# A norm, local attention, norm and gated feed-forward layer: one rank for every step, attention weights divided before they are spread, and five norms named for transposes by DMA

## The chip, the cores and the metric

The kernel runs on one core of a Trainium2 chip. The metric is the time of one execution on the device in microseconds (us); before the change the median of five runs is 211.15 us (211.06 to 212.95). A core has a matmul engine (TensorE, PE in the profile; PEld is its loading of weights), a vector engine (VectorE, DVE), an engine for activation functions and copies (ScalarE, ACT), GpSimd (POOL) and a queue engine (SyncE, SP) that issues DMAs. Each executes its own instructions in order and waits for the others by semaphores. Matmuls write to PSUM, which has eight banks of 128 partitions by 512 fp32 values; all other tiles lie in SBUF.

## What is computed

The input `x` has 2048 positions of width 512. The layer is pre-norm attention, then a pre-norm gated feed-forward, each with a residual. B_x is not used.

```python
h  = x + A(layernorm(x))
h2 = h + B(layernorm(h))

# A: 32 heads of width 16; each position attends to 8 positions: itself, 2 back, ... 14 back
q, k, v = split(x @ wqkv)
logits = einsum("bhsd,bhswd->bhsw", q, kg) * 16**-0.5     # kg, vg: k, v at s - 2*w
attn = softmax(where(s - 2*w >= 0, logits, -1e9))
A = einsum("bhsw,bhswd->bhsd", attn, vg) @ wo

# B: F = 1376
gate = x @ W_gate; gate = gate * (gate > 0)
B = (gate * (x @ W_up)) @ W_down
```

Data are bf16; layernorm has no weights and an epsilon of 1e-5.

## The kernel before

The positions are cut into four chunks of 512 (`tk` 0 to 3), each of four blocks of 128 rows. Row-wise work (norms, residuals, output) has positions on the partitions, all other work has features on the partitions and the 512 positions along the free dimension, so each norm's output is transposed. A chunk passes through these steps:

- **Norm of x** (`layernorm`, L400): DVE takes mean and variance of each block (L429, L432), ACT makes the reciprocal deviation by Ln and Exp (L442, L446), then DVE (chunk 0) or ACT (L484) writes the normed block. Four PE transposes a block write to PSUM (L494, 16 for a norm), and two ACT copies for a chunk bring two blocks each to SBUF (L512; one of chunk 0 is on DVE, L510). A second branch of the function transposes by DMA from SP (`f_td`, four transfers a block); it is entered on the test `(ln, tk) in DMAT` at L458, where `ln` is "x" or "h" and `tk` the chunk, and `DMAT` is the empty tuple.
- **Projections**: twelve groups of four matmuls (L544) for q, k and v, each drained by ACT (L552). In chunk 0 the first two groups are cut in half-widths, so that they can start on half the rows.
- **Scores**: DVE multiplies q with four shifted views of k for two feature tiles at a time (L591, four instructions a chunk). Eight small matmuls sum within heads (L597, four groups a chunk). ACT takes the exponential (L606), four window positions in each of two tiles; in chunk 0 DVE zeroes what lies before the start (L609).
- **Weights**: the undivided exponentials are spread by PE from a head to its features (L625, two groups of four) and copied by ACT to SBUF (L632, eight). Beside this two matmuls give the sums (L639), and ACT makes their reciprocal by Ln (L642) and Exp (L645).
- **Values**: for each of four feature tiles DVE multiplies the eight spread weights with shifted views of v (L662), adds eight to one in three steps (L665) and multiplies with the reciprocal (L669, tile `rec`).
- **Output product and residual**: four groups of four matmuls (L700); DVE adds each to x and keeps the sum of each row (L705).
- **Norm of h**: from these sums (L414), ACT's square sums (L420), Ln, Exp, DVE (L487), transposes as above.
- **Feed-forward**: 11 feature tiles, the last of 96; for each four matmuls for up and four for gate (L727), two ACT drains (L731, L734), a DVE product for two tiles (L747). Then for each block 11 matmuls in two parts of 8 and 3 (L759), a DVE addition of h (L763) and a store from SP.

The order is not the program's. Each step is added to a `Plan` (L168) with an engine, an estimated duration, its dependencies and the buffers that it takes. `Plan.order` (L189) then makes the order before the kernel is built: for each engine it collects the steps that could start soonest, within a small window (`LOOK`: 0.05 us for PE, 0.3 DVE, 0.1 ACT), and takes the one with the smallest priority. The priorities come from the table `PRIO`: one number for each kind of step and chunk (L182). Buffers are given out in the same pass: 8 PSUM banks for all uses, 9 tiles `quad` for normed, projected and attended data, 5 tiles `big` for products and weights. The engines receive their steps in the resulting order and keep it.

Input loads are issued in a fixed order in `setup`: x of chunk 0 (half from SP, half from ACT), the three projection weights, x of chunk 1, wo, up and gate weights, x of chunks 2 and 3, the down weights. While the first rows load, 54 matmuls on zeros (`NWARM`, L522) keep PE busy.

Of the kernel before, what the change touches and what calls it, by code (L numbers as in the profile page):

```python
# [8 lines left out]
P = 128  # L9
# [8 lines left out]
PRIO = {  # L18
    "warm": (329, 0, 0, 0),
    "xst": (-357, -495, 2394, -54),  # L20
    "xag": (-520, -862, -182, 1996),
    "xrl": (-362, -296, 194, 2166),
    "xre": (-82, 283, 2306, 886),
    "xxn": (-286, 2378, 367, 2013),
    "xtp": (540, 1594, 641, 716),
    "xte": (-646, 2834, 2727, 2443),
    "qkh0": (442, 0, 0, 0),
    "qkv0": (418, 417, 1697, 353),
    "qe0": (1262, 2340, 2135, 2291),
    "qkh1": (1644, 0, 0, 0),  # L30
    "qkv1": (449, 1372, 2578, 2742),
    "qe1": (2915, 2429, 2602, -366),
    "qkv2": (352, 2556, 1012, 1671),
    "qe2": (2725, 402, 863, 106),
    "qkv3": (453, 1501, 226, 815),
    "qe3": (2462, 2595, 2528, 2174),
    "qkv4": (1443, 695, 1687, 267),
    "qe4": (-122, 2839, 177, 2325),
    "qkv5": (701, 873, 594, 1878),
    "qe5": (-44, -211, -170, 2493),  # L40
    "qkv6": (862, 1457, 638, 395),
    "qe6": (-199, -327, 2260, -230),
    "qkv7": (487, 427, 68, 358),
    "qe7": (402, 2319, 2485, -311),
    "qkv8": (1720, 1667, 1519, 453),
    "qe8": (2802, 2488, 2656, 114),
    "qkv9": (1851, -242, 2722, 391),
    "qe9": (1309, 2749, 876, 2302),
    "qkv10": (1764, 857, 1851, 1678),
    "qe10": (2412, 1400, 2395, 458),  # L50
    "qkv11": (2427, 1522, 1794, 722),
    "qe11": (2598, 2825, -204, 2326),
    "pr0": (-482, 1697, -427, 2119),
    "sc0": (1698, 2659, 1551, 1498),
    "ex0": (2396, 2052, 1825, -25),
    "mk0": (2108, 0, 0, 0),
    "pr1": (-469, 1768, -500, 2606),
    "sc1": (404, 855, 418, 1193),
    "ex1": (1517, 142, -363, 143),
    "mk1": (-591, 0, 0, 0),  # L60
    "bc0": (1924, 469, 3082, 309),
    "be0": (-60, -227, 44, 2335),
    "bc1": (-281, 491, 1693, 187),
    "be1": (-373, 324, 2173, 119),
    "den": (1891, 635, 1806, 811),
    "dl": (2476, 2727, -37, 2595),
    "dr": (2494, 2236, 2409, 3002),
    "mu0": (-490, -741, -300, -559),
    "tree0": (-169, -269, -240, -508),
    "om0": (1670, 1359, 1810, -68),  # L70
    "mu1": (-422, -682, -366, -477),
    "tree1": (-140, -329, -243, -384),
    "om1": (-229, -267, 2395, -350),
    "mu2": (-555, -491, 2098, -268),
    "tree2": (-170, 1809, -660, 904),
    "om2": (-521, 1855, -320, -517),
    "mu3": (-551, 1681, 1796, 1815),
    "tree3": (-437, 1819, -540, 1964),
    "om3": (1672, 1855, -287, 2080),
    "wo0": (627, 1946, 489, 2577),  # L80
    "rs0": (-246, -458, -830, -312),
    "wo1": (438, 583, 385, 3140),
    "rs1": (-643, 2078, 1855, 2067),
    "wo2": (313, 69, 182, 553),
    "rs2": (-732, -369, -32, 1663),
    "wo3": (1166, 959, 49, 924),
    "rs3": (-414, -240, 1839, -148),
    "hnm": (-209, -423, 2603, -326),
    "hsq": (2388, 2706, 2324, -39),
    "hrl": (-604, -445, 2636, -334),  # L90
    "hre": (2395, -231, 2261, 2466),
    "hxn": (-412, -519, -293, -471),
    "htp": (609, 1635, 1868, 152),
    "hte": (1320, 2163, 155, 494),
    "mm0": (1484, 427, 528, 389),
    "ue0": (-673, 2837, 2251, 2336),
    "ge0": (44, 2326, -675, 97),
    "gu0": (2058, -433, -474, -124),
    "mm1": (823, 1820, 930, -289),
    "ue1": (1892, 191, 2067, -310),  # L100
    "ge1": (2639, 225, 2423, 2049),
    "gu1": (-496, -252, 1690, -742),
    "mm2": (-16, 412, 2609, 908),
    "ue2": (2776, 2713, -363, 2679),
    "ge2": (-65, 2678, 2266, 2262),
    "gu2": (2019, -373, -285, 1530),
    "mm3": (1801, -279, -278, 2624),
    "ue3": (2151, 164, 2100, 2147),
    "ge3": (-79, 2604, 224, -393),
    "gu3": (-491, -577, -568, 1516),  # L110
    "mm4": (471, 1194, -255, 2655),
    "ue4": (109, 43, 210, 2788),
    "ge4": (2240, 2269, 103, 3043),
    "gu4": (-304, -564, 2366, -656),
    "mm5": (88, 1884, 2524, 706),
    "ue5": (121, -114, 1286, 1403),
    "ge5": (-228, 2600, -52, 2852),
    "gu5": (-362, -366, 1055, 1556),
    "dn0": (415, 2726, 1868, 1679),
    "o0": (-185, 2463, -169, 1484),  # L120
    "os0": (-1500, -1424, -1612, -1426),
    "dn1": (438, 584, 2860, -448),
    "o1": (-495, -599, 1809, 1682),
    "os1": (-1609, -1383, -1616, -1425),
    "dn2": (1621, 2632, 1892, 368),
    "o2": (1891, -170, 2256, 1030),
    "os2": (-1268, -1189, -1208, -1424),
    "dn3": (2453, 2779, 469, 3112),
    "o3": (2772, 2257, -622, -485),
    "os3": (-1239, -1323, -1444, -1438),  # L130
    "xnb": (0, -605, -729, -589),
}
# [35 lines left out]
class Plan:  # L168
# [9 lines left out]
    def add(self, key, *a, **k):  # L178
        op = Op(*a, **k)
        op.key = key  # L180
        if key and key[0] in PRIO:
            op.prio = PRIO[key[0]][key[1]]  # L182
        op.seq = len(self.ops)
        self.ops.append(op)
        for b in set(op.take) | set(op.use):
            b.left += 1
        return op
# [57 lines left out]
def kernel(  # L245
# [18 lines left out]
    W = 8  # L264
# [26 lines left out]
    spread = sb.tile([P, P], BF16, name="spread")  # L291
    mask = sb.tile([P, 2, PADL], BF16, name="mask")
# [37 lines left out]
    sel_i, sp_i, mk_i = ints[:, 0:H], ints[:, H:H + P], ints[:, H + P:H + P + PADL]  # L330

    def setup():

        w3_r = A_wqkv.rearrange("(dt p) f -> p dt f", p=P)
        nc.sync.dma_start(x_sm[:, 0:2, :], x_rows[:, 0:2, :])
        nc.scalar.dma_start(x_sm[:, 2:4, :], x_rows[:, 2:4, :])
        for c, q in enumerate((nc.sync, nc.scalar, nc.sync)):
            q.dma_start(w3_sb[c][:], w3_r[:, :, c * D:(c + 1) * D])
        nc.sync.dma_start(x_sm[:, BPC:2 * BPC, :], x_rows[:, BPC:2 * BPC, :])
# [4 lines left out]
        for tk in range(2, NCK):  # L344
            nc.sync.dma_start(x_sm[:, tk * BPC:(tk + 1) * BPC, :], x_rows[:, tk * BPC:(tk + 1) * BPC, :])
# [11 lines left out]
        nc.gpsimd.iota(sp_i[:], pattern=[[1, H], [0, DQ]], base=0, channel_multiplier=0)  # L357
        nc.gpsimd.iota(mk_i[:], pattern=[[1, PADL]], base=0, channel_multiplier=0)
# [10 lines left out]
        V.tensor_scalar(out=spread[:], in0=sp_i[:], scalar1=cf[:, 1:2], scalar2=None, op0=ALU.is_equal)  # L369
        for hf in range(2):  # L370
            V.tensor_scalar(out=mask[:, hf, :], in0=mk_i[:], scalar1=cf[:, 2 + hf:3 + hf],
                            scalar2=None, op0=ALU.is_ge)
# [7 lines left out]
    NWARM = 54  # L380
    DMAT = ()
# [12 lines left out]
    xload = [None] * NCK  # L394
    for tk in range(NCK):
        xload[tk] = add(None, "LD", 0.0, None, lat=[3.3, 11.0, 22.0, 24.0][tk])
    wload = {n: add(None, "LD", 0.0, None, lat=v) for n, v in
             (("q", 5.7), ("k", 7.0), ("v", 8.5), ("o", 12.5), ("u", 16.5), ("g", 20.5), ("d", 28.0))}

    def layernorm(tk, src, dst_slots, pr, groups, on_act, residual=None):  # L400
# [7 lines left out]
        for grp in groups:  # L408
            ag, xns = [], {}
            lo, hi = grp[0], grp[-1] + 1  # L410
            for j in grp:
                if residual:
# [6 lines left out]
                    def f_sq(j=j, xn=xns[j]):  # L419
                        nc.scalar.activation(out=xn.t[:], in_=x_sm[:, tk * BPC + j, :], func=ACT.Square,  # L420
                                             bias=mv.t[:, j, 0:1], scale=1.0, accum_out=sq.t[:, j:j + 1])

                    a = add((ln + "nm", tk), "DVE", DSM, f_nm, [src[j]], pr, take=[mv], use=[sm], lat=DL)
                    ag.append(add((ln + "sq", tk), "ACT", AX + 0.2, f_sq, [a], pr, take=[sq, xns[j]], use=[mv], lat=AL))
                else:
# [8 lines left out]
                    a = add((ln + "st", tk), "DVE", DST, f_st, [src[j]], pr, take=[st], lat=DL)  # L434
                    ag.append(add((ln + "ag", tk), "DVE", DSM, f_ag, [a], pr, take=[mv], use=[st], lat=DL))

            def f_ln(lo=lo, hi=hi):
# [3 lines left out]
                else:  # L441
                    nc.scalar.activation(out=rs.t[:, lo:hi], in_=mv.t[:, lo:hi, 1], func=ACT.Ln,  # L442
                                         bias=eps_t[:, 0:1], scale=1.0)
# [10 lines left out]
            l = add((ln + "rl", tk), "ACT", AS, f_ln, ag, pr, take=[rs], use=[sq or mv], lat=AL)  # L454
            e = add((ln + "re", tk), "ACT", AS, f_ex, [l], pr, use=[rs], lat=AL)
            if on_act:
                e = add((ln + "nb", tk), "DVE", DSM, f_nb, [e], pr, take=[nb], use=[mv, rs], lat=DL)
# [69 lines left out]
    for tk in range(NCK):  # L527
# [49 lines left out]
        for hf in range(2):  # L577
# [38 lines left out]
            exd.append(a)  # L616


        ab, abd = Buf(big_s), []
        for hf in range(2):  # L620
            bcs = [Buf(at_s) for _ in range(4)]

# [195 lines left out]
```

## Time and profile before

| What | us |
|---|---|
| Median of five runs | 211.15 |
| Profiled execution | 211.12 |
| its span in the profile | 209.3 |
| PE busy in the span | 198.6 (95%) |
| DVE busy | 169.4 (81%) |
| ACT busy | 137.7 (66%) |
| First projection matmul starts | 9.55 |
| First feed-forward matmul of chunk 0 starts | 74.3 |
| Last matmul ends | 205.9 |

The granted clock of TensorE is 1.00 throughout. A matmul's busy time in the profile is from its first read to its last write, 379 ns for 512 columns; consecutive ones overlap, and one starts every 0.216 us. Busy PE time is therefore not work at full rate, and small gaps between matmuls don't show in it.

### The profile page before, as it was taken

How to read it: one execution, taken by the hardware profiler on the slowest of the kernel's cores; microseconds unless marked ns; L12 is line 12 of the kernel's file. 1: busy time of each engine (PE TensorE's matmuls, PEld its weight loads, DVE VectorE, ACT ScalarE, POOL GpSimd, SP SyncE). 2: the span in 40 equal slices, each digit the busy share in tenths (PEclk: the TensorE clock that was granted, in tenths of full speed). 3: DMA queues.
4: the chain of work that ended last, by engine and by line, in shares of the span. 5: the costliest groups of instructions: out<-in, count | busy, mean ns of one | idle time of the engine just before them, and what ended most of it. 6: DMA issues, size and time to landing. Idle time of an engine off the chain costs nothing.

```text
span 209.3 us, 2987 instructions
## 1 busy us (share of the span) xinstructions
PE 198.6 (95%) x1142; PEld 96.0 (46%) x1142; DVE 169.4 (81%) x253; ACT 137.7 (66%) x262; POOL 1.6 (1%) x13
## 2 busy tenths in 40 slices
PE   8699899999998799999999999999999999999993
PEld 8464345554543344444354444444444445444441
DVE  5799999999998999999999999859999972122024
ACT  2369999979798887449776643677654644666210
POOL 3000000000000000000000000000000000000000
PEclk9999999999999999999999999999999999999999
DMA  6999800000000000000000000000000002000003
GB/s 207 359 400 375 266 9 2 0 0 0 3 0 0 0 3 0 0 0 3 0 27 25 0 30 0 8 17 28 0 25 0 25 28 75 0 0 2 3 21 105
DMA packets 8638, 10.71 MB, mean 51 GB/s; under 512 B 464, under 2 KB 7472, under 8 KB 8624
## 3 DMA queue, kind: packets, MB, share of 16 engines
q1 hardware_dynamic: 7824, 9.73, 13.5%
q10 hardware_dynamic: 800, 0.79, 1.1%
q8 instruction: 9, 0.15, 0.3%
q14 instruction: 5, 0.04, 0.1%
HBM read 8.42 MB, written 2.10 MB: 50 GB/s over the span
## 4 chain that ended last, share of the span: by engine, by line
PE 69%; DVE 24%; issue 2%; ACT 2%; DMA 2%; DVEq 0%; ACTq 0%
PE bank L727 36%; PE bank L759 18%; DVE big L591 8%; PE bank L700 5%; PE bank L544 5%; DVE big L665 4%; DVE big L662 4%; DVE st L429 3%; PE bank L494 2%; PE bank L597 2%; DMA x_sm<-in_A_x_dram 2%; DVE x_sm L705 1%; ACT quad L512 1%; DVE row L487 1%; DVE mv L432 1%
## 5 line engine op out<-in xcount | busy, mean ns | idle before, releaser
L727 PE MATMUL bank<-quad,wu_sb 128*128 128x512 bf16 (+1 forms) x176 | 45.2, 379 | 0.0
L727 PE MATMUL bank<-quad,wg_sb 128*128 128x512 bf16 (+1 forms) x176 | 45.2, 379 | 0.0
L759 PE MATMUL bank<-wd_sb,gT 128*128 128x512 bf16 (+1 forms) x176 | 40.5, 379 | 0.0
L731 ACT CAST up_sb<-bank 128x512 bf16<-128x512 f32 (+1 forms) x44 | 25.6, 586 | 18.8 <-PE bank L727 12.2
L665 DVE TENSOR_TENSOR big<-big 128x2048 bf16<-128x2048 bf16 (+2 forms) x48 | 37.0, 777 | 1.0
L734 ACT ACTIVATE gr<-bank 128x512 bf16<-128x512 f32 (+1 forms) x44 | 26.1, 600 | 16.0 <-PE bank L727 13.1
L591 DVE TENSOR_TENSOR big<-quad,kT 128x4096 bf16<-128x4096 bf16 x16 | 35.9, 2282 | 0.7 <-ACT kT L552 0.7
L662 DVE TENSOR_TENSOR big<-big,vT 128x4096 bf16<-128x4096 bf16 x16 | 36.3, 2285 | 0.0
L747 DVE TENSOR_TENSOR gT<-gr,up_sb 128x1024 bf16<-128x1024 bf16 (+1 forms) x24 | 15.2, 641 | 25.6 <-ACT gr L734 25.4
L727 PEld LDWEIGHTS <-wu_sb 128*128 128x128 bf16 (+1 forms) x176 | 17.5, 100 | 20.8 <-issue 0.8
L727 PEld LDWEIGHTS <-wg_sb 128*128 128x128 bf16 (+1 forms) x176 | 17.6, 100 | 20.4
L759 PEld LDWEIGHTS <-gT 128*128 128x128 bf16 (+1 forms) x176 | 16.7, 98 | 20.2 <-issue 1.3
L632 ACT CAST big<-bank 128x512 bf16<-128x512 f32 x32 | 16.6, 626 | 2.3 <-PE bank L625 2.3
L512 ACT COPY quad<-bank 128x1024 bf16<-128x1024 bf16 x15 | 14.8, 1033 | 5.0 <-PE bank L494 5.0
L544 PE MATMUL bank<-quad,wv_sb 128*128 128x512 bf16 x64 | 16.2, 381 | 0.7 <-ACT quad L512 0.7
L544 PE MATMUL bank<-quad,wq_sb 128*128 128x512 bf16 (+1 forms) x68 | 15.7, 366 | 0.6 <-ACT quad L512 0.6
L544 PE MATMUL bank<-quad,wk_sb 128*128 128x512 bf16 (+1 forms) x68 | 15.7, 367 | 0.0
L420 ACT ACTIVATE row<-x_sm,mv 128x512 bf16<-128x512 bf16 x16 | 11.5, 732 | 5.3 <-DVE mv L414 5.3
L700 PE MATMUL bank<-wo_sb,quad 128*128 128x512 bf16 x64 | 14.7, 379 | 0.4 <-DVE quad L669 0.4
L763 DVE TENSOR_TENSOR row<-x_sm,bank 128x512 bf16<-128x512 bf16 x16 | 10.8, 684 | 4.7 <-PE bank L759 3.2
L429 DVE BATCH_NORM_STATS2 st<-x_sm 128x6 f32<-128x512 bf16 x16 | 10.5, 670 | 2.0 <-DMA x_sm<-in_A_x_dram 2.0
L597 PE MATMUL bank<-big,sel 128*32 128x512 bf16 x128 | 9.7, 384 | 2.5 <-DVE big L591 2.5
(55 smaller groups left out, 157.0 us busy)
## 6 DMA issues: line engine op xcount, KB each, us to landing
out_dram<-row SPq DMA_DIRECT2D x16, 128.0 KB, 1.7
x_sm<-in_A_x_dram SPq DMA_DIRECT2D x3, 512.0 KB, 15.3
wu_sb<-in_B_W_up_dram SPq DMA_DIRECT2D x1, 1376.0 KB, 13.6
wg_sb<-in_B_W_gate_dram SPq DMA_DIRECT2D x1, 1376.0 KB, 16.4
wd_sb<-in_B_W_down_dram SPq DMA_DIRECT2D x1, 1280.0 KB, 17.7
wq_sb<-in_A_wqkv_dram SPq DMA_DIRECT2D x1, 512.0 KB, 5.6
wk_sb<-in_A_wqkv_dram ACTq DMA_DIRECT2D x1, 512.0 KB, 7.3
wv_sb<-in_A_wqkv_dram SPq DMA_DIRECT2D x1, 512.0 KB, 7.5
```

Source lines behind the costliest of these rows:

```text
L429: V.bn_stats(out=st.t[:], in_=x_sm[:, tk * BPC + j, :])
L512: nc.scalar.copy(out=o, in_=i)
L544: nc.tensor.matmul(mm.t[:, lo:hi], lhsT=w3_sb[c][:, dt, t:D:NT], rhs=xnT.t[:, dt, lo:hi], start=(dt == 0), stop=(dt == NT - 1))
L591: V.tensor_tensor(out=pb.t[:].rearrange("p (t w) s -> p t w s", t=2), in0=q4, in1=k4, op=ALU.mult)
L632: nc.scalar.copy(out=ab.t[:, w, :], in_=bc.t[:])
L662: V.tensor_tensor(out=mt.t[:], in0=ab.t[:], in1=v8, op=ALU.mult)
L665: V.tensor_tensor(out=mt.t[:, 0:n, :], in0=mt.t[:, 0:n, :], in1=mt.t[:, n:2 * n, :], op=ALU.add)
L700: nc.tensor.matmul(od.t[:], lhsT=OT.t[:, t, j * P:(j + 1) * P], rhs=wo_sb[:, t, :], start=(t == 0), stop=(t == NT - 1))
L727: nc.tensor.matmul(mm.t[:fs, :], lhsT=w_sb[:, dt, ft * P: ft * P + fs], rhs=hnT.t[:, dt, :], start=(dt == 0), stop=(dt == NT - 1))
L731: nc.scalar.copy(out=ub.t[:fs, i, :], in_=um.t[:fs, :])
L734: nc.scalar.activation(out=gr.t[:fs, i, :], in_=gm.t[:fs, :], func=ACT.Relu)
L759: nc.tensor.matmul(od.t[:], lhsT=gts[ft].t[:fs, ft % 2, j * P:(j + 1) * P], rhs=wd_sb[:fs, ft, :], start=(ft == 0), stop=(ft == NFT - 1))
```

## The change

- `DMAT` becomes `("x2","x3","h0","h1","h2")`. The branch's test at L458 stays as it is, and so do the four transfers of `f_td`. The common code that makes a normed block becomes `norm(j)`, used by both branches.
- The priorities become `RANK`: 753 numbers, each from 0 to 752 once, one for each step in the order in which steps are added.
- `EARLY = (1, 2, 3)`: in these chunks the sums are made with a matrix `same`, which leaves one sum for each head and window position in the layout of the exponentials; after Ln and Exp two DVE multiplies (`am`) divide the two tiles of exponentials in place, and only then are they spread. The four multiplies L669 fall away, and the last addition of a tree writes the attended tile itself. Chunk 0 keeps the old way.
- `RPE = (0,)`: in chunk 0 a fifth matmul with the identity adds x in the output product, and ACT, not DVE, drains the four results with their row sums; the square sums then read PSUM. `OPE`, `MERGE` and `BCN` add further options whose values keep the old way.
- Chunk 0's start: x is loaded in four transfers of one block, in turn from SP and ACT; norm groups are [0, 1], [2], [3]; the last block's mean and variance are made by two ACT passes with sums (`xsu`, `xsq`); each block is transposed and copied out on its own, two on ACT and two on DVE; four projection groups are cut in half-widths, not two. 48 matmuls warm PE, not 54.
- x of chunks 1 to 3 is loaded before wo and the feed-forward weights.
- In the last chunk the fourth block's down product, addition and store are made in two halves of 256 columns.
- Some estimated durations and load times of the plan change with this.

```diff
-PRIO = {
-    "warm": (329, 0, 0, 0),
...
+RANK = [
+    0, 1, 2, 3, 4, 5, 6, 7, 8, 9, 10, 11, 12, 13, 14, 17, 19, 15, 18, 22,
...
-        if key and key[0] in PRIO:
-            op.prio = PRIO[key[0]][key[1]]
         op.seq = len(self.ops)
+        if RANK:
+            op.prio = RANK[op.seq]
...
-        nc.sync.dma_start(x_sm[:, 0:2, :], x_rows[:, 0:2, :])
-        nc.scalar.dma_start(x_sm[:, 2:4, :], x_rows[:, 2:4, :])
+        for j in range(BPC):
+            (nc.scalar if j % 2 else nc.sync).dma_start(x_sm[:, j:j + 1, :], x_rows[:, j:j + 1, :])
...
-        nc.sync.dma_start(x_sm[:, BPC:2 * BPC, :], x_rows[:, BPC:2 * BPC, :])
+        for tk in range(1, NCK):
+            nc.sync.dma_start(x_sm[:, tk * BPC:(tk + 1) * BPC, :], x_rows[:, tk * BPC:(tk + 1) * BPC, :])
...
-    NWARM = 54
-    DMAT = ()
+    NWARM = 48
+    DMAT = ("x2","x3","h0","h1","h2")
+
+    EARLY = (1, 2, 3)
+
+    RPE, OPE = (0,), ()
+
+    MERGE = ()
+
+    BCN = 4
...
+                elif tk == 0 and j == BPC - 1:
...
+                    def f_su(j=j, xn=xns[j], sm=sm):
+                        nc.scalar.activation(out=xn.t[:], in_=x_sm[:, j, :], func=ACT.Copy,
+                                             accum_out=sm.t[:, j:j + 1])
...
             if (ln, tk) in DMAT:
                 for j in range(lo, hi):
-                    xn = xns.get(j) or Buf(xn_s)
...
+                    xn, a = norm(j)
 
                     def f_td(j=j, xn=xn):
                         for t in range(NT):
                             nc.sync.dma_start_transpose(out=dst.t[:, t, j * P:(j + 1) * P],
                                                         in_=xn.t[:, t * P:(t + 1) * P])
...
-        groups = [[0, 1], [2, 3]] if tk == 0 else [[0, 1, 2, 3]]
+        groups = [[0, 1], [2], [3]] if tk == 0 else [[0, 1, 2, 3]]
...
+        if tk in EARLY:
+            for hf in range(2):
+                def f_am(ex=exs[hf], rc=rc):
+                    V.tensor_tensor(out=ex.t[:], in0=ex.t[:], in1=rc.t[:], op=ALU.mult)
+
+                exd[hf] = add(("am%d" % hf, tk), "DVE", D2, f_am, [rcd], apr + 1, use=[exs[hf], rc], lat=DL)
...
+                if tk in RPE:
+                    nc.tensor.matmul(od.t[:], lhsT=identity[:], rhs=x_sm[:, tk * BPC + j, :],
+                                     start=False, stop=True)
...
+                if tk in RPE:
+                    nc.scalar.activation(out=r, in_=od.t[:], func=ACT.Copy, accum_out=sm.t[:, j:j + 1])
...
+        parts = [(j, 0, D) for j in range(BPC)]
+        if tk == NCK - 1:
+            parts[-1:] = [(BPC - 1, 0, D // 2), (BPC - 1, D // 2, D)]
```

## The prediction

> **What bounds the kernel now.** I read the chain that ended last first, then its pieces in order of time, then the busy time by stretch, and the costliest groups last. The chain by engine and five of its pieces (start, length, what):
>
> ```profile
> PE 69%; DVE 24%; issue 2%; ACT 2%; DMA 2%; DVEq 0%; ACTq 0%
> ```
>
> ```profile
> 9.55 7.95 PE bank L544 x44
> ...
> 70.13 1.38 DVE row L487 x4
> ...
> 73.76 0.61 PE bank L597 x8
> 74.38 19.10 PE bank L727 x88
> ...
> 205.92 0.69 DVE row L763
> ```
>
> PE is the chain from 9.55 to about 23 us, DVE from there to 73.76, and PE again, without a gap, until 205.9. So the kernel has two halves. They meet where chunk 0's second norm is transposed (the four L487 at 70.13) and its feed-forward matmuls start (74.38; their weights load from 74.31). I call that moment T0; it is 74.3 now. The same by stretch (length, then busy us and count of PE, weight loads, DVE, ACT, POOL, then granted clock):
>
> ```profile
> 9.50:26.00 16.50, 15.67 (x115) 8.42 (x115) 15.10 (x21) 13.32 (x25) 0.00 (x0) 1.00 0.99 354
> 26.00:59.00 33.00, 32.09 (x172) 16.72 (x171) 32.55 (x50) 30.15 (x59) 0.00 (x0) 1.00 0.01 2
> 59.00:74.30 15.30, 12.67 (x124) 4.81 (x122) 14.59 (x11) 13.52 (x29) 0.00 (x0) 1.00 0.00 0
> 74.30:110.00 35.70, 35.70 (x190) 16.14 (x187) 35.20 (x49) 24.75 (x51) 0.00 (x0) 1.00 0.02 5
> ```
>
> Between 9.5 and 74.3, that is in 64.8 us, DVE is busy 62.2, ACT 57.0 and PE 60.4, with overlapping ends counted as busy. After T0 PE is full. A gain is therefore either an earlier T0, or less PE work after T0, or a shorter end. The groups that price the edits:
>
> ```profile
> L494 PE MATMUL bank<-identity,row 128*128 128x128 bf16 x128 | 10.3, 220 | 1.9 <-DVE row L487 1.6 <-ACT row L484 0.3
> L512 ACT COPY quad<-bank 128x1024 bf16<-128x1024 bf16 x15 | 14.8, 1033 | 5.0 <-PE bank L494 5.0
> L705 DVE SCALAR_TENSOR_TENSOR x_sm<-x_sm,bank 128x512 bf16<-128x512 bf16 x16 | 10.4, 678 | 0.0
> L420 ACT ACTIVATE row<-x_sm,mv 128x512 bf16<-128x512 bf16 x16 | 11.5, 732 | 5.3 <-DVE mv L414 5.3
> L669 DVE TENSOR_TENSOR quad<-big,rec 128x512 bf16<-128x512 bf16 x16 | 6.2, 419 | 0.2
> ```
>
> Back to back they cost less than their mean: sixteen transposes take 0.89 us in the chain, an L669 0.34, an L705 0.61, an L591 or L662 2.20 (13.29 for six), a tree of three L665 2.32, an L429 with its share of L432 0.69, an L420 with its accumulator read 0.72 (54.58 less 53.86).
>
> **The DMA transposes: I count them at nothing.** The branch asks `(ln, tk) in DMAT`, a pair such as ("h", 0); DMAT becomes a tuple of strings such as "h0", so no pair is ever found. The list of ranks agrees: it holds 753 numbers, and counting the steps that the changed code adds gives 753 with every norm on PE, but 743 with five norms on DMA (per norm 8 steps for four rows in place of 10). Only with 753 does every rank lie after the ranks of what it depends on. So the 80 transposes (80 × 0.0557 = 4.5 us of PE) and ten L512 stay, and SP gets no new issue. Were the branch taken, that row would promise −4.5 us, and a rule speaks against it: the Trainium skill, "VectorE: DVE Perf Modes", section "The three transpose paths", gives 390 ns on TensorE but 1309 ns by the DMA crossbar for one 128×128 tile. Sixteen in a row would be an estimated 20.9 us where PE and L512 now need 2.6 (70.82 to 73.4); chunk 0's norm alone would move T0 by 18 us. No row here shows such a transfer.
>
> **Before T0.** DVE sets the floor. From the landing of chunk 1's rows (10.8) to the last of the four L487, DVE now does 12 L591 (26.4), 4 L662 (8.8), 4 trees (9.3), 4 L669 (1.35), 12 statistics (8.8), 4 L705 (2.4), and small ones (2.1): 59.2, and ends at 71.5, so 1.5 idle. By the ranks, the changed kernel does before that point 13 L591 (+2.2), two multiplies by the reciprocal for chunk 1 (+0.7), no L705 for chunk 0 (−2.4), and batches its statistics (−0.5): 59.2 again. Of the 1.5 idle, 0.3 waited for the mask's exponentials and 0.7 for a kT eviction; the ranks put other products ahead of both, so I keep 0.6. The four L487 then end at 10.8 + 59.2 + 0.6 = 70.6, and with the 2.8 us that now lie between them and T0, T0 = 73.4.
>
> The first chunk's new start (rows loaded singly on two queues, one row's statistics on ACT as two passes of 0.72, half-width products for four outputs rather than two) brings the first projection from 9.55 to about 8.8. DVE waits for chunk 1's rows anyway (0.9 us at 10.79, same bytes ahead of them), so I count it at nothing; x of chunks 2 and 3 ahead of the later weights delays those by 1 MB, 2.7 us at 375 GB/s, against a first need at 48.9 for wo: nothing.
>
> ACT pays. To the same point it gains chunk 0's four residual drains with sums, one exponential (0.5) and one Ln/Exp pair (1.05), and loses one L632 and two L552 (−1.5). A drain has no row; near it are a plain PSUM exponential (614 ns) and L420 with its read (0.72 back to back). Bounds are 0.5 and 0.8 each; I take 0.72, 2.9 in all. Here a rule weighs against the change too: the Trainium skill, "ScalarE: Activation LUTs", section "Rules for kernel authors", puts add and multiply on VectorE, up to about three times faster in bf16. By that rule the four would cost 7.3 (3 × 2.4); the row has L705, which reads fp32 PSUM, at 0.61, so the move costs 0.1 apiece. ACT's 57.0 become 60.0 (64.4 by the rule, which would leave it no wait at all).
>
> PE gets four residual matmuls in chunk 0 (4 × 0.217 = 0.87). They lie before T0, where PE has 4.4 us without work now: hidden, 0.87 if that cover goes. 48 warm matmuls for 54 end 0.6 earlier, in a gap.
>
> **After T0.** PE's remaining 131.6 us keep their contents, except that by rank one product group of L597 (0.55) and one of L639 less L625's one more (0.1) now go before T0: 131.0. Divided weights turn four L669 of a chunk into two multiplies (−0.7 of DVE per chunk in chunks 1 to 3) and put sum, Ln, Exp and multiply ahead of the spreading: 0.43 + 0.5 + 0.55 + 0.34 and hops, some 2.2 us. For chunk 1 DVE has three L591 to do (6.6), for chunk 2 the residuals and second norm of chunk 1, for chunk 3 a whole feed-forward: covered; uncovered, 2.2 each. The place to watch is chunk 1's output product. From the L487s on, DVE has 3 L591, 4 L662, 4 trees, a multiply and five L747: 27.8, so it is ready at T0 + 25.0. PE has ahead of it 88 matmuls, two first parts of L759, two L597 groups and one L625: 23.9. The last quarter enters only with the fourth matmul, 0.65 later: 1.1 − 0.65, say 0.5 us of PE idle (0 to 1.1). For chunks 2 and 3 the same count leaves DVE 1 us and more ahead: 21.2 against 22.0 from the norm's end, and 2.3.
>
> **The end.** The last output is halved: its L763 takes about 0.42 for 0.69, and 64 KB land a little sooner than 128 KB: 3.0 for 3.4.
>
> **Sum.** 73.4 + 131.0 + 0.5 + 3.0 = 207.9 of span, against 209.3. The profiled execution took 211.12, 1.8 more than its span, and the median is 211.15: 207.9 + 1.8 = 209.7.
>
> **The rivals.** *The idle only moves* (same): T0 stays at 74.3 because 1.5 us of DVE idle return, for instance at the four L487 waiting for ACT's square sums; 74.3 + 131.0 + 1.0 + 3.0 = 209.3, 211.1. For it: all three engines are over 88% busy before T0. Against: the two waits named above lose their cause. *ACT becomes the bound* (slower): with 60.0 us of work from 9.5, and the 7.8 us of waits of now less the 1.0 that the earlier first projection saves, ACT reaches T0 at 76.3: 76.3 + 131.0 + 0.5 + 3.0 = 210.8, 212.6. It decides from T0 = 74.8 on, when ACT waits more than 5.3 us. For it: PSUM banks wait on ACT, and the drained banks of chunk 0 are held until they are squared. Against: much of ACT's waiting was for PE, which had slack. *The DMA branch is taken after all*: +18 at T0 less 4.5 of PE, about 224 or more.
>
> **How the numbers follow.** What can be told from no change is 0.5%, 1.05 us. Forecast 0.48, idle moves 0.24, ACT bound 0.27, DMA 0.01. The forecast's own range runs from the floor (no idle, T0 72.0, no stall: 206.0, so 207.8) to 210.6. For 8 in 10 I take 207.2, a little below the floor for the durations' own scatter, to 213.2, which takes in the ACT case. Faster 0.48, same 0.24, slower 0.28.
>
> **What would show it.** Right: 128 matmuls of the transposing line and no transfer but loads and 16 or 17 outputs; T0 near 73.4 with PE full behind it save half a us at chunk 1's output product; L705's line 12 times on DVE; first projection near 8.8. Wrong: transposing transfers on SP; ACT the last to finish before T0; gaps of PE of over 1 us after T0, or a T0 below 72, which would mean that DVE's work was not the floor.

## The result, and the profile after

The changed kernel takes 210.1 us (median of 20 runs, 209.0 to 210.72) against 211.17 (39 runs of the kernel before beside them): a ratio of 0.9928, 95% interval 0.9910 to 0.9946. That is 0.7% faster by the ratio, and 0.4 us above the 209.7 forecast. The ratio compares means: 15 of the 39 executions of the kernel before took over 212 us, which the medians (0.5% apart) don't show. The sum came out nearly as forecast, but its terms did not.

The chain that ended last, by engine, from the page of the kernel after:

```profile
PE 69%; DVE 13%; ACT 10%; DMA 5%; issue 2%; SPq 1%; DVEq 0%; ACTq 0%
```

And its pieces in order of time (start, length, what):

```profile
2.66 9.82 DMA x_sm<-in_A_x_dram
12.51 2.47 DVE st L390 x4
...
61.16 1.16 ACT x_sm L692 x4
62.32 1.45 ACT big L622 x3
...
70.81 1.45 ACT big L622 x3
72.26 0.50 ACT ex L571
72.76 1.82 ACT quad L470 x2
...
74.62 6.20 PE bank L721 x28
...
195.81 9.56 PE bank L758 x55
...
205.39 0.42 DVE row L769
```

Three things are new beside the chain of before. It begins with a load: chunk 1's rows land at 12.5 us where they landed at 10.8, and DVE's statistics (L390) start with them. Its last stretch before the feed-forward runs over ACT, where it ran over DVE: drains of chunk 0's residual (L692) and of spread weights (L622), then the copies of the transposed norm (L470). And the last addition is half as wide. T0 is 74.62 for 74.31, 1.2 us later than forecast. PE ends at 195.81 + 9.56 = 205.37. The stretches (columns as before: length; busy us and count of PE, weight loads, DVE, ACT, POOL; clock; DMA share; GB/s):

```profile
9.50:26.00 16.50, 14.79 (x106) 9.32 (x106) 13.49 (x24) 12.30 (x24) 0.00 (x0) 1.00 1.04 370
26.00:59.00 33.00, 32.59 (x210) 15.68 (x209) 32.90 (x35) 30.57 (x56) 0.00 (x0) 1.00 0.02 7
59.00:74.60 15.60, 14.66 (x113) 6.33 (x112) 14.91 (x17) 15.01 (x37) 0.00 (x0) 1.00 0.01 1
74.60:110.00 35.40, 35.38 (x190) 15.84 (x190) 32.45 (x45) 24.56 (x50) 0.00 (x0) 1.00 0.02 8
```

The first stretch is the thin one: DVE is busy 13.49 us of 16.50, where it was 15.10. From 26 on it has no gap worth a name. ACT's busy time from 9.5 to T0 is 12.30 + 30.57 + 15.01 = 57.9, not the 60.0 of the forecast. The groups that the change touches, and the loads at the start (size, time from issue to landing):

```profile
L470 ACT COPY quad<-bank 128x1024 bf16<-128x1024 bf16 (+1 forms) x16 | 15.1, 1000 | 6.8 <-PE bank L456 6.7
L456 PE MATMUL bank<-identity,row 128*128 128x128 bf16 x128 | 9.8, 220 | 1.1 <-DVE row L425 1.1
L694 DVE SCALAR_TENSOR_TENSOR x_sm<-x_sm,bank 128x512 bf16<-128x512 bf16 x12 | 8.2, 684 | 3.0 <-PE bank L683 3.0
L692 ACT ACTIVATE x_sm<-bank 128x512 bf16<-128x512 f32 x4 | 2.6, 652 | 0.0
```

```profile
wq_sb<-in_A_wqkv_dram SPq DMA_DIRECT2D x1, 512.0 KB, 7.7
x_sm<-in_A_x_dram SPq DMA_DIRECT2D x2, 128.0 KB, 3.0
```

All 128 transposes are still matmuls and no norm goes by DMA. The residual is on DVE twelve times and on ACT four. The first weights take 7.7 us to land, where before they took 5.6:

```profile
wq_sb<-in_A_wqkv_dram SPq DMA_DIRECT2D x1, 512.0 KB, 5.6
```

Where the 1.1 us of span came from, term by term: T0 +0.3; PE work after T0 from 131.6 to 205.37 − 74.62 = 130.75, −0.85; the end from 3.4 to 2.84, −0.55. Nothing came from an earlier T0.

### The profile page after: what moved, and what is told of

Its sections match the earlier page's. It is cut to its first block, busy times and chain, and to the rows that moved or that the text cites. A ratio compares the mean times of both kernels' runs of the same rounds, so it can differ in the third digit from the quotient of the medians.

```text
span 208.2 us, 3004 instructions
## 1 busy us (share of the span) xinstructions
PE 199.6 (96%) x1159; PEld 98.5 (47%) x1159; DVE 162.1 (78%) x241; ACT 139.1 (67%) x277; POOL 1.8 (1%) x14
## 4 chain that ended last, share of the span: by engine, by line
PE 69%; DVE 13%; ACT 10%; DMA 5%; issue 2%; SPq 1%; DVEq 0%; ACTq 0%
PE bank L721 37%; PE bank L758 18%; PE bank L683 5%; DMA x_sm<-in_A_x_dram 5%; PE bank L502 4%; DVE big L640 4%; ACT big L622 4%; DVE big L637 3%; DVE big L549 2%; DVE st L390 2%; PE bank L456 2%; PE bank L555 2%; ACT row L360 1%; ACT x_sm L692 1%; ACT quad L470 1%
## 5 line engine op out<-in xcount | busy, mean ns | idle before, releaser
L721 PE MATMUL bank<-quad,wu_sb 128*128 128x512 bf16 (+1 forms) x176 | 42.1, 379 | 0.5 <-ACT quad L470 0.5
L721 PE MATMUL bank<-quad,wg_sb 128*128 128x512 bf16 (+1 forms) x176 | 41.6, 379 | 0.0
L758 PE MATMUL bank<-wd_sb,gT 128*128 128x512 bf16 (+3 forms) x187 | 40.4, 367 | 0.0
L728 ACT ACTIVATE gr<-bank 128x512 bf16<-128x512 f32 (+1 forms) x44 | 25.8, 602 | 16.3 <-PE bank L721 10.8
L640 DVE TENSOR_TENSOR big<-big 128x2048 bf16<-128x2048 bf16 (+2 forms) x36 | 31.1, 892 | 0.2
L758 PEld LDWEIGHTS <-gT 128*128 128x128 bf16 (+1 forms) x187 | 17.9, 98 | 19.2 <-issue 0.7
L769 DVE TENSOR_TENSOR row<-x_sm,bank 128x512 bf16<-128x512 bf16 (+1 forms) x17 | 10.8, 652 | 15.9 <-PE bank L758 15.9
L470 ACT COPY quad<-bank 128x1024 bf16<-128x1024 bf16 (+1 forms) x16 | 15.1, 1000 | 6.8 <-PE bank L456 6.7
L622 ACT CAST big<-bank 128x512 bf16<-128x512 f32 x32 | 17.4, 633 | 0.8 <-PE bank L616 0.8
L390 DVE BATCH_NORM_STATS2 st<-x_sm 128x6 f32<-128x512 bf16 x15 | 9.5, 680 | 3.8 <-DMA x_sm<-in_A_x_dram 3.8
L510 ACT CAST quad<-bank 128x512 bf16<-128x512 f32 x16 | 9.7, 613 | 2.7 <-PE bank L502 2.7
L425 DVE TENSOR_SCALAR row<-x_sm,mv,rs 128x512 bf16<-128x512 bf16 x20 | 7.0, 408 | 5.6 <-ACT rs L407 5.6
```

What stands on the lines that cost most here:

```text
L470: nc.scalar.copy(out=o, in_=i)
L622: nc.scalar.copy(out=ab.t[:, w, :], in_=bc.t[:])
L640: V.tensor_tensor(out=mt.t[:, 0:n, :], in0=mt.t[:, 0:n, :], in1=mt.t[:, n:2 * n, :], op=ALU.add)
L721: nc.tensor.matmul(mm.t[:fs, :], lhsT=w_sb[:, dt, ft * P: ft * P + fs], rhs=hnT.t[:, dt, :], start=(dt == 0), stop=(dt == NT - 1))
L728: nc.scalar.activation(out=gr.t[:fs, i, :], in_=gm.t[:fs, :], func=ACT.Relu)
L758: nc.tensor.matmul(od.t[:, c0:c1], lhsT=gts[ft].t[:fs, ft % 2, j * P:(j + 1) * P], rhs=wd_sb[:fs, ft, c0:c1], start=(ft == 0), stop=(ft == ...
```

## Experiments

Three theories on T0. *Late rows*: the four small transfers of chunk 0's rows delay what is loaded behind them, and DVE carries chunk 1's late rows to T0. *ACT*: the drains moved to ACT set T0, as the chain suggests. *Order*: T0 comes from the planned order, and single edits are swallowed. Line numbers in an experiment can be shifted.

### Chunk 0's rows in two transfers again

```diff
-        for j in range(BPC):
-            (nc.scalar if j % 2 else nc.sync).dma_start(x_sm[:, j:j + 1, :], x_rows[:, j:j + 1, :])
+        nc.sync.dma_start(x_sm[:, 0:2, :], x_rows[:, 0:2, :])
+        nc.scalar.dma_start(x_sm[:, 2:4, :], x_rows[:, 2:4, :])
```

> Kernel after, with x of chunk 0 loaded in two transfers of 256 KB again; order unchanged. Late-rows theory (chunk 1's rows land at 12.5 us instead of 10.8 because of the four small transfers, and chunk 0's second half of the way waits for that): rows at about 10.8, T0 about 73.2, time 1.2 to 1.5 us below after's 210.1. ACT theory (the four residual drains on ACT set T0): rows at about 10.8, T0 still 74.4 to 74.8, time within 0.4 of 210.1. Order theory (T0 comes from the planned order, and single changes of a few tenths are swallowed): T0 moves by less than half of what the rows gain, time 209.3 to 209.9.

Measured: 208.56 us (208.35 to 209.15), ratio to before 0.9857 (0.9822 to 0.9892), so 1.5 us below the kernel after. Pieces of its chain:

```profile
2.28 8.43 DMA x_sm<-in_A_x_dram
10.73 2.47 DVE st L390 x4
...
72.85 6.20 PE bank L721 x28
...
194.03 9.56 PE bank L758 x55
```

Rows 1.78 us earlier (12.51 less 10.73), T0 1.77 earlier, last matmul 1.78 earlier: everything is shifted as one block. From rows to T0 both kernels need 62.1 us. What the small transfers do is seen in what the DMAs moved in the first 26 us, in slices of 0.65 us, first after, then this kernel:

```profile
GB/s 0 0 36 251 270 254 167 187 238 307 323 312 345 386 383 337 369 359 353 361 366 390 388 405 381 408 402 411 406 415 406 406 387 392 372 357 352 350 303 176
```

```profile
GB/s 0 0 28 143 348 374 377 351 339 318 358 364 364 353 353 347 348 345 350 389 429 359 394 402 406 406 407 411 406 406 406 398 373 356 355 349 353 337 123 44
```

With four transfers the rate falls to 167 to 238 GB/s in slices seven to nine, between the rows and the weights behind them; with two it stays at 339 and more. The same bytes lie ahead of chunk 1's rows; they move later. By a sum of the slices (an estimate) that is 1.1 of the 1.8 us: 2.98 MB had moved here when the rows landed, and the kernel after gets that far at 11.8 us. Its rows land only at 12.5, with 3.22 MB moved, so transfers behind them had taken a share. Late rows holds; the other two fall.

### The same part alone, on the kernel before

The opposite edit in the kernel before: only its two transfers become four.

> Kernel before with one part of the change alone: x of chunk 0 in four transfers of one block. Late-rows theory: chunk 1's rows land at 12.3 to 12.8 for 10.8, and DVE, which waits for them, carries it to T0: T0 75.6 to 76.2, time 212.5 to 213.2. If DVE of the kernel before has slack enough to swallow it: 211.2 to 211.7.

Measured: 212.44 us (211.38 to 214.78), ratio 1.0033 (1.0005 to 1.0061). The chain of the profiled execution:

```profile
2.66 9.98 DMA x_sm<-in_A_x_dram
12.66 0.70 DVE st L429
...
75.74 19.10 PE bank L727 x88
```

Rows 1.9 us later, T0 1.4 later, 1.2 in the median: this part alone makes the kernel before slower. The median lies a little under the range. (The ratio shows less, as five of the 16 executions of the kernel before beside it ran at a mean clock of 0.99; see the last section.)

### Chunk 0's residual back on DVE

`RPE = ()`. The list of ranks still fits step for step; the planner's order shifts a little with the durations.

> Kernel after, with chunk 0's residual back on DVE: no identity matmuls (PE -0.87 before T0), four L705 forms on DVE (+2.4), none of the four drains on ACT (-2.6). ACT theory: T0 comes 1 to 2 us earlier than 74.6, time 208.1 to 209.1. Late-rows theory (DVE is the floor from its late start): T0 goes 1.5 to 2.4 us later, time 211.6 to 212.5. Order theory: in between, T0 within 1 us of 74.6.

Measured: 211.37 us (210.04 to 211.84), ratio 0.9979 (0.9953 to 1.0005).

```profile
12.87 2.47 DVE st L390 x4
...
76.19 6.15 PE bank L721 x28
```

From rows to T0 it now takes 76.19 − 12.87 = 63.3 us for 62.1. Taking the drains off ACT and giving their work to DVE makes T0 later, so ACT was not the bound, though the chain runs over ACT for its last 15 us. DVE's 2.4 us more work costs only half of itself: 0.7 comes back because DVE no longer waits for ACT's last drain, and 0.5 because the transposed norm is copied sooner (T0 comes 2.9 us after the last L425 for 3.4). The move is worth 1.2 us in this order. The ACT theory falls; the late-rows theory's figure for this run was a little too high.

TensorE's granted clock was 0.50 from 9.3 to 12.6 in this execution and 1.00 in the kernel after. That is not the cause: DVE waits for its rows until 12.87 anyway, and the profiled execution of the next run had the same dip and still took the 62.1 (74.82 − 12.70).

### The last block in one piece

The two lines that halve the last block's output are taken out.

> Kernel after, with the last block's addition and store in one piece again. All theories: the end after the last matmul is 3.3 to 3.4 again for 2.84, T0 and the matmuls after it unchanged; time 0.4 to 0.6 us above after's 210.1, so 210.5 to 210.7. If the halved end gave nothing, 210.1.

Measured: 210.19 us (209.63 to 211.3), ratio 0.9938 (0.9911 to 0.9966). The timed runs can't tell it from the kernel after. The profile can, in the last of these pieces of its chain:

```profile
12.70 2.47 DVE st L390 x4
...
74.82 6.20 PE bank L721 x28
...
205.55 0.69 DVE row L767
```

The last matmul ends at 205.53 and the span at 208.8: an end of 3.27 for 2.84. The halved end is worth 0.4 us by the profile, unproved by the times.

### The norms really by DMA

The test becomes `if ln + str(tk) in DMAT:`, and ranks are looked up by the step's name (a DMA transpose takes the rank of the PE transpose that it replaces).

> Kernel after, with the test mended so that the five named norms really are transposed by DMA from SBUF to SBUF (80 fewer matmuls, ten fewer ACT copies, 80 more transfers issued by SP). The prediction's rival: one transposing transfer of 128 x 128 takes an estimated 1.3 us and they queue up, T0 some 18 us later, total about 224 or more. The other side, if the transfers go side by side on the 16 DMA engines at the plan's own estimate of 4.5 us a block: T0 within 4 us of 74.6, PE 3 us less work after T0, total 208 to 212.

Measured: 290.44 us, ratio 1.372. One line each of the DMA issues, of the transposing line (duration of an issue, min/median/max) and of the waits:

```profile
quad<-row SPq DMA_TRANSPOSE x80, 2.3
```

```profile
L518 SPq DMA_TRANSPOSE quad<-row x80: 1093/1230/1615, 28.8 to 219.5; - x80
```

```profile
PE bank L797 <- DMA quad<-row: 41.6, 12, 14.7
```

Each transpose keeps SP's queue for 1.23 us, and the next follows it; sixteen are 19.7, plus 2.3 to land. T0 is 118.9, 44 us later, not the 18 of the prediction: PE executes in order, and it stands before chunk 2's and chunk 3's projections too (the longest waits there 6.0 and 12.5 us), which lie ahead of T0, then 9.0 at T0. The estimate of one norm was near, the count was not: (290.4 − 210.1) / 5 = 16.1 us for each of five norms. PE's waits for these transfers sum to 64.0 of the 80.3 us (L797 41.6, the projections L578 22.4). Where PE stands, its granted clock falls to 0.50 for a time (0.85 in the mean of the run), which may account for the other 16; the two weren't separated. The prediction's "about 224 or more" counted one norm and the saved PE time. That the branch isn't entered is what keeps this change from being a loss.

### Division late in every chunk, and the order alone

`EARLY = ()`, with chunk 0's rows in two transfers and ranks by name:

> Kernel after with x of chunk 0 in two transfers (208.56 us, rows of chunk 1 at 10.7, T0 72.85), and EARLY empty: weights are divided after spreading in every chunk, as before the change; ranks go by the step's name. By the prediction's working: two multiplies (0.7) leave DVE's way to T0, so T0 72.1 to 72.9; 0.7 more DVE work a chunk after T0 is covered; time 207.8 to 208.7. If dividing early is itself worth something (DVE pressed after T0): gaps of PE of 0.5 to 2 us after T0, time 209.0 to 210.5.

Measured: 211.35 us (210.9 to 214.32), ratio 1.0012 (0.9982 to 1.0043), that is 2.8 above the same kernel with early division, and beyond both expectations. The three executions at a clock of 0.998 or more took 210.9 to 211.2, so the clock is not the reason. Its pieces and PE's waits after T0:

```profile
73.08 6.20 PE bank L797 x28
...
99.16 3.45 PE bank L759 x16
...
197.03 9.56 PE bank L834 x55
```

```profile
PE bank L797 <- ACT quad L546: 1.9, 2, 1.4
PE bank L532 <- DVE row L501: 1.0, 1, 1.0
```

T0 stays (73.08 for 72.85), but PE's stretch behind it grows from 194.03 + 9.56 − 72.85 = 130.74 to 133.51. Chunk 1's output product (L759) starts at T0 + 26.1; with early division it starts at 97.19, T0 + 24.3. PE then stands at chunk 1's second norm, for DVE's rows and ACT's copies. On ACT, four drains of spread weights (L698) now stand in front of the norm's last square sum (L436), and four more in front of those copies:

```profile
104.33 2.05 ACT L698 CAST big<-bank 128x512 bf16<-128x512 f32 x4
106.25 0.76 ACT L436 ACTIVATE row<-x_sm,mv 128x512 bf16<-128x512 bf16 x1
```

With early division the last square sum (at 102.20) comes before the drains (104.10). To tell the late product from the drains, the spreading was held back by a dependency on the reciprocal that it doesn't use:

> The kernel that divides late in every chunk (211.35 us), with one dependency more: in chunks 1 to 3 the spreading also waits for the reciprocal, which it doesn't use; nothing is divided early. In the profile without it PE stands for 2.8 us after T0, because ACT's drains of spread weights go in front of chunk 1's second norm. Holding theory (dividing early is worth something only because it holds the spreading back): PE after T0 130.7 to 131.2, time 208.4 to 209.3. Multiplies theory (two multiplies for four, and one step fewer behind each tree, make the gain): the stall stays, 210.9 to 211.4.

Measured: 211.98 us (211.66 to 214.43), ratio 1.0050 (1.0032 to 1.0067). The clock of the profiled execution is 0.95 between 110 and 180 us, so only its waits before 120 us are used:

```profile
PE bank L797 <- ACT quad L546: 2.0, 2, 1.5
PE bank L532 <- DVE row L501: 1.1, 1, 1.1
```

The same stall at the same place, and a time above both ranges. But the dependency did not clear ACT's queue: four drains still begin at 103.94, in front of the last square sum at 105.84. So it shows only that this dependency doesn't mend the stall, and does not tell the two causes apart. DVE's work between T0 and chunk 1's output product is one: four multiplies (4 × 0.34 = 1.4 us) that early division has turned into two ahead of T0, which would fit most of the 1.8 us by which the product starts later. The drains in front of the last square sum (2.05 us) are the other. That late division costs 2.8 us with these ranks is shown; the share of each cause is not.

Then the new order without any of the edits, in the kernel before:

> Kernel before with nothing of the change but the order: every step that both kernels have takes the rank that it has after (the added multiplies, identity matmuls, ACT drains, halves and loads are left out). Order theory (the new order closes the idle time of DVE before T0 and moves a group of PE work ahead of it): T0 lies 62 to 63.5 us behind chunk 1's rows at 10.8, so 72.8 to 74.3, PE work after it 130.7 to 131.0, end 3.4: 208.7 to 210.4. Edits theory (the moved residual and the divided weights make the gain, the order alone does nothing): T0 74.3 or later, time 211.0 or more.

Measured: 223.69 us (223.31 to 224.04), ratio 1.0583 (1.0553 to 1.0613). Both expectations were wrong, and by far.

```profile
PE bank L499 <- ACT big L637: 4.8, 1, 4.8
...
DVE big L667 <- issue: 4.0, 1, 4.0
```

```profile
58.14 7.36 PE bank L549 x24
```

PE stands 4.8 us behind the drains of spread weights and DVE 4.0 in front of its first product with v. Chunk 2's projections start at 58.14 behind that wait and end at 75.8; in the kernel before they ran from 52.3 to 66.5. T0 is 83.06. A part of this is the clock: after PE has stood from 50.35, it is 0.50 from 52.0 to 62.3, and the transposes and projections there take up to twice their time.

```profile
26.00:59.00 33.00, 26.83 (x181) 12.87 (x180) 28.91 (x28) 29.77 (x56) 0.00 (x0) 0.89 0.01 2
```

That is an estimated 2.8 us: 0.8 on sixteen transposes (1.87 for 1.07 at full clock) and 2.0 on twelve projection matmuls (4.60 for 12 × 0.216). The order is not good or bad in itself: it is fitted to the edits, and loses 12.5 us without them, this loss of clock with it.

### Chunk 1's rows ahead of the v weights

If T0 follows chunk 1's rows, they should come sooner still. Two transfers for chunk 0, then:

```diff
         for c, q in enumerate((nc.sync, nc.scalar, nc.sync)):
+            if c == 2:
+                q.dma_start(x_sm[:, BPC:2 * BPC, :], x_rows[:, BPC:2 * BPC, :])
             q.dma_start(w3_sb[c][:], w3_r[:, :, c * D:(c + 1) * D])
```

> Kernel after with x of chunk 0 in two transfers, and x of chunk 1 issued ahead of the v weights instead of behind them; order unchanged. Late-rows theory carried on (T0 follows chunk 1's rows): 512 KB fewer ahead of them, 1.4 us at 375 GB/s, so rows at 9.3 to 9.5, T0 71.4 to 71.7, time 207.1 to 207.4. PE theory (from 8.8 to 33 us PE has only 0.6 us without work, so PE takes over as the bound there): T0 0.4 to 0.8 us earlier, time 207.8 to 208.2. If the v weights now come late: they land at about 10.7 and are first read at 15.7, so nothing.

Measured: 208.68 us (207.45 to 209.38), ratio 0.9865 (0.9830 to 0.9900): no gain in the median. Two executions took 207.45 and 207.59, the others 208.66 and more; the profile is of one of these:

```profile
6.00:7.50 1.50, 0.25 (x4) 0.26 (x4) 1.09 (x5) 1.40 (x7) 0.00 (x0) 0.95 1.09 364
7.50:9.00 1.50, 1.50 (x16) 1.46 (x15) 1.30 (x5) 0.58 (x1) 0.00 (x0) 0.50 1.10 350
9.00:10.50 1.50, 1.50 (x9) 1.07 (x8) 1.50 (x4) 0.58 (x1) 0.00 (x0) 0.50 1.10 348
```

TensorE's granted clock is 0.50 from about 7.4 us on, just as the transposes (7.25) and the first projections (8.90) begin. The 48 warm matmuls had ended at 5.2, and PE had no work until 7.25. So:

> The kernel of the last run (x of chunk 1 ahead of the v weights, x of chunk 0 in two transfers) with 58 warm matmuls for 48, nothing else moved. In its profile PE was busy 0.97 us of the three from 4.5 to 7.5 and ran at a granted clock of 0.50 from 7.5 to about 10.9, 3.4 us at half speed. Gap theory (the thin use of PE before 7.5 brings the half clock): the ten more matmuls fill 0.6 to 1.1 us of it, the clock stays at 1.00, T0 71.6 to 72.0, median 207.3 to 207.6. If the half clock comes whatever PE does there: median stays at 208.6 to 208.8. If the added matmuls run into the first transposes at 7.3: 0.2 to 0.5 later than 207.5.

Measured: 207.59 us (207.55 to 207.61), ratio 0.9815 (0.9782 to 0.9847).

```profile
6.00:7.50 1.50, 0.41 (x9) 0.24 (x5) 1.09 (x5) 1.47 (x8) 0.00 (x0) 1.00 1.10 350
7.50:9.00 1.50, 1.47 (x19) 1.04 (x17) 1.42 (x6) 0.87 (x2) 0.00 (x0) 1.00 1.10 350
```

> As the run beside it, with 64 warm matmuls. Gap theory: clock 1.00 too; 16 more matmuls are 0.9 us at 56 ns and 1.7 us at the 107 ns that they take in the first microseconds, so where they run slow they end at about 8.0 and hold the first transposes up by 0.6: median 207.4 to 208.1. If the half clock comes anyway: 208.6 or more.

Measured: 207.61 us (207.54 to 207.66), ratio 0.9816 (0.9783 to 0.9849). With ten more warm matmuls the mean clock is 0.999 or more in every execution and the scatter falls to 0.06 us; six more change nothing. This version beats both kernels: 1.85% below before by the ratio, and 2.5 us below after. DVE starts on chunk 1 at 8.97, without waiting, 1.76 us earlier than with two transfers alone, but T0 is 71.82, only 1.03 earlier: the chain no longer begins with chunk 1's rows but runs over PE's first projections (of the version with 58), as the PE theory had it, at a price between the two forecasts:

```profile
8.71 4.52 PE bank L504 x32
...
71.82 6.20 PE bank L723 x28
```

## Why the prediction was right, and where it was not

- **T0 = 73.4: wrong, 74.62.** The failed step is "DVE waits for chunk 1's rows anyway (0.9 us at 10.79, same bytes ahead of them), so I count it at nothing". The bytes were the same; the transfers were not. The rows landed at 12.5, and with two transfers at 10.7, T0 at 72.85. Worth 1.5 us of time.
- **DVE's floor: right in kind, two sizes off.** From rows to the last L425 (at 71.22) DVE is busy 57.9 of 58.7 us, for 59.2 and 0.6 idle: −1.1. About half of it is the batched statistics: their groups take 8.6 us (L390, L393) for 9.7 (L429, L432), which is 1.1 less and not 0.5. From there to T0 it took 3.4 for 2.8, because the transposes' copies wait behind three L622 and an exponential on ACT. Rows +1.7, floor −1.1, this +0.6: the +1.2.
- **The residual on ACT: mis-sized upward.** A drain with its sum takes 0.59 where it follows another step directly ("63.77 0.59 ACT x_sm L692 x2" in the chain), for 0.72, so it equals DVE's 0.61. The rule of the Trainium skill that was weighed there (ScalarE: Activation LUTs, Rules for kernel authors) gives its factor for bf16; with this fp32 PSUM source the four drains took 2.4 us and not the 7.3 worked out from it. ACT's busy time grew by 0.9, not 3.0.
- **First projection at 8.8: wrong at 9.38, right at 8.76 with two transfers.** It was the late q weights, not the norm.
- **After T0: 131.0 right (130.75).** The matmuls that went ahead of T0 are those that were counted: L597 and L639 fewer, L625 four more. The half us of stall at chunk 1's output product didn't come: it started at T0 + 24.3, a little before the forecast's T0 + 25.0. That it is the place to watch was right: without early division it costs 2.8.
- **End 3.0: 2.84.**
- **DMA transposes at nothing: right.** Its rival's price for one norm was right too (sixteen in an estimated 20.9 us, 19.7 plus 2.3 measured), but it counted one norm where five pay.
- **The rivals.** "The idle only moves" describes T0 best by number (74.3), but not by cause. "ACT becomes the bound" did not come: it was to decide from T0 = 74.8, and the run without ACT's drains was slower.
- **The range's floor.** Its T0 of 72.0 doesn't follow from the terms: 10.8 + 59.2 + 2.8 = 72.8, which puts the floor's time at 208.6 and not 207.8.

So the time was right by luck: 1.7 us of late rows, which weren't in the sum, stood against 1.4 us that the other terms had too much (by the kernel with two transfers: a span of 206.5 for 207.9). What each edit is worth in the order of before was tested for the four transfers alone.

## What to carry to other kernels

When the first half of a kernel hangs on an engine that starts with a load, look at the landing of that load, not at the bytes ahead of it: here cutting an earlier transfer in four cost more than it brought, and the shift went through to the end unchanged. A chain that runs over an engine doesn't say that this engine sets the time; take its work away before you believe it. An order computed for one set of steps belongs to that set: alone it lost 12.5 us, and without early division 2.8. And look at the granted clock of the profiled execution before you compare two profiles.

## What the runs showed of the hardware

- Four transfers of 128 KB on two queues moved 251 to 270 GB/s, and the next weights came through a dip at 167 to 238; two of 256 KB went over into the weights at 339 to 377 GB/s. Why the rate dips is not shown.
- A transposing DMA from SBUF to SBUF of 128×128 bf16 holds its issuing queue for 1.23 us and lands 2.3 us after issue; transposes on one queue don't overlap their issues.
- TensorE can lose half its clock for 3.4 us (7.35 to 10.8 in the run with chunk 1's rows ahead), or for three times as long (52.0 to 62.3 with the order alone), in some executions of one kernel and not in others. The length of the gap in PE's work does not decide it: the loss came after 2.0 us without a matmul (5.2 to 7.25) and after 1.4 (8.2 to 9.5, the last block in one piece), while 1.6 us (6.1 to 7.7) passed at 1.00 in the kernel before. The Trainium skill (TensorE: Matmul & The Clock Gate, What's actually happening) gives a free-running window of 3.4 us, which fits the lengths and the scatter. Its rule against gaps of over about 3.4 us (the same page, HAM oscillation — how this bites in real kernels) would have passed the two short ones; the measurement decides. Ten warm matmuls more were worth 1.1 us in the median.
- What the loss costs depends on what else is late. Of 65 executions of the kernel before beside the experiments, the 17 at a mean clock of 0.989 to 0.992 took 212.05 to 212.98 us and the other 48 took 210.95 to 211.36. The kernel after had such a clock in 8 of 20 and took 210.06 to 210.68, the others 209.0 to 210.72, so it loses little by it. That fits its DVE waiting for rows until 12.5, and a gain that is larger by the means than by the medians.
